# Attention weights turned in front of the last pair's values and copied behind its first four products

## The chip, the cores and the metric

The kernel runs on one core of a Trainium2 chip. Its engines work side by side, each through its own queue in order: TensorE (PE in the rows; PEld are its weight loads), VectorE (DVE), ScalarE (ACT), GpSimd (POOL) and SyncE (SP), which here only issues DMAs. TensorE writes to PSUM; VectorE and ScalarE read PSUM and write SBUF. The metric is the device time of one execution in microseconds, median of several runs.

## What is computed

Three stages on fp32 data: attention that is causal by blocks of 64, for 4 x 8 heads of 576 positions with 64 features; a two-layer network with a leaky ReLU; and a mixture of eight experts whose gate is normalised eight times by rows and columns. The change touches the attention alone:

```python
batch, n_heads, seq, head_dim = (4, 8, 576, 64)

def _attn_ref(q, k, v):
    B, H, S, D = q.shape
    block = 64
    scale = 1.0 / np.sqrt(D)
    scores = scale * np.matmul(q, k.transpose(0, 1, 3, 2))
    pos = np.arange(S)
    mask = pos[:, None] // block >= pos[None, :] // block
    scores = np.where(mask, scores, -1000000000.0)
    scores = scores - np.max(scores, axis=-1, keepdims=True)
    attn = np.exp(scores)
    attn = attn / (np.sum(attn, axis=-1, keepdims=True) + 1e-09)
    return np.matmul(attn, v).astype(np.float32)
```

## The kernel before

The attention works on pairs of heads: 16 pairs, 128 partitions each (two heads of 64). `attention` runs a loop over pairs p from -1 to 16, and in it over the nine query blocks i in the order 8, 7, 0, 6, 1, 5, 2, 4, 3 (`turn_order`). In turn p it works for several pairs at once: the scores of pair p+1, the turning of the weights of pair p, the values of pair p-1, and the loading and turning of q and k for the pairs behind.

- **Score i** (`score`, L323 to L332): one matmul `sc` of 64(i+1) keys (two halves of 288 for score 8), its row maximum on VectorE (`nmax`), and its exponential on ScalarE (`ex`) with the row sum, which is read out by a second short instruction. The PSUM pool of the scores has three buffers. There are ten score matmuls in a turn, so each takes the buffer of the one three before it, once that one's exponential is through.
- **Turning the weights** (`turn_attn`, L358 to L372): the 25 blocks of 128 keys by 128 (two heads of 64 queries) of `ex` are transposed in seven groups, 0 to 6, of four blocks (one in group 6), into a PSUM tile `tr`, and each group is copied into the SBUF tile `at`. Groups 0, 3 and 5 are copied by ScalarE, groups 1, 2, 4 and 6 by VectorE (for pair 15: 0, 2, 4, 6 by ScalarE). Turned q (`qm`), k (`km`) and their tails (`qk_tail`) use the same three PSUM buffers as `tr`. There is one `at` for all pairs.
- **Values** (`weigh`, L385 and L388): twelve products of v with `at`, two heads side by side, into `av`. The first four (all with key chunk 0) read the blocks of groups 0 and 1 and the first of group 2; the other eight read groups 2 to 6.
- **split_x** (L396 to L406): VectorE multiplies `av` by the reciprocal row sums into `xs`; ScalarE casts `xs` to `xh` (two casts for the four pairs whose rows lie in two tiles), and GpSimd takes the rest into `xl`.

The copy of group 0 of pair p overwrites what the first products of pair p-1 have read, so it comes behind them. In the table `beside`, which says what else is written down beside each score, the values, `split_x` and `turn_attn` of group 0 stand beside score 7, groups 1 and 2 beside scores 0 and 6, group 3 beside score 2, group 4 beside 4, and groups 5 and 6 beside 3.

TensorE executes in the order in which the code is written down. On the other engines the scheduler of the framework sets the order from the same code. In the first 15 turns five steps each of preparing the first layer's weights (`bits_steps`, L154 to L202) are mixed in, on VectorE, ScalarE and GpSimd. Everything behind the attention (matmuls at L499, L519, L775, L829) is untouched.

Of the kernel before, what the change touches and what calls it, by code (L numbers as in the profile page):

```python
# [8 lines left out]
F32 = mybir.dt.float32  # L9
# [6 lines left out]
P = 128  # L16
BLK = 64
# [19 lines left out]
def block_attention_mlp_moe(  # L37
# [177 lines left out]
    def attention(att, ps_sc, ps_tr, ps_av):  # L215
        qraw = att.tile([P, NFULL, P], F32, name="qraw")
        kraw = att.tile([P, NFULL, P], F32, name="kraw")
# [16 lines left out]
        order = [(i, c) for c in range(NKC) for i in range(2 * c, NQ)]  # L234
# [115 lines left out]
        def spread_totals(p):  # L350
            with ExitStack() as queued:
                queued.enter_context(tc.issue_after(getattr(fetched[0], "ins", fetched[0])))
                for h in range(2):
                    nc.sync.dma_start(
                        out=by_feature[p % 2][h * D:(h + 1) * D, :], in_=rows[p][h:h + 1, :].to_broadcast([D, S])
                    )

        def turn_attn(p, g):  # L358
            todo = order[4 * g:4 * g + 4]
            n = len(todo)  # L360
            tr = ps_tr.tile([P, 4, 2, BLK], F32, name="tr", tag="tr")
            for s, (i, c) in enumerate(todo):
                nc.tensor.transpose(  # L363
                    tr[:, s].rearrange("p h q -> p (h q)"),
                    ex[p % 2][:, off[i] + c * P:off[i] + (c + 1) * P],
                    ident,
                )
            dst = at[:, 4 * g:4 * g + n]
            if g in ((0, 3, 5) if p + 1 < NP else (0, 2, 4, 6)):
                nc.scalar.copy(out=dst, in_=tr[:, 0:n])  # L370
            else:
                nc.vector.tensor_copy(out=dst, in_=tr[:, 0:n])  # L372
# [20 lines left out]
        def split_x(p):  # L393
# [16 lines left out]


        tails_far = [("far", load_tail, qraw, q), ("far", load_tail, kraw, k)]
        values = [("prv", weigh, 0, h, part) for part in range(2) for h in range(2)]
        values += [("prv", weigh, c, h, 1) for c in range(1, NKC) for h in range(2)]
        beside = {
            8: [("fol", turn_q), ("far", load_rows, qraw, q)],
            7: [("fol", turn_k), ("far", load_rows, kraw, k), *values, ("prv", split_x), ("cur", turn_attn, 0)],
            0: [("cur", turn_attn, 1)],
            6: [("cur", turn_attn, 2), ("nxt", load_v)],
            1: [],  # L420
            5: [("fol", turn_tail), *tails_far],
            2: [("cur", turn_attn, 3)],
            4: [("cur", turn_attn, 4), ("cur", spread_totals)],
            3: [("cur", turn_attn, 5), ("cur", turn_attn, 6)],
        }
        turn_order = [8, 7, 0, 6, 1, 5, 2, 4, 3]

# [95 lines left out]
    with (  # L523
        tc.tile_pool(name="att", bufs=1) as att,
        tc.tile_pool(name="ps_sc", bufs=3, space=bass.MemoryType.PSUM) as ps_sc,
        tc.tile_pool(name="ps_tr", bufs=3, space=bass.MemoryType.PSUM) as ps_tr,
        tc.tile_pool(name="ps_av", bufs=1, space=bass.MemoryType.PSUM) as ps_av,
    ):
        with tc.manual_schedule(engines={mybir.EngineType.PE}):
            attention(att, ps_sc, ps_tr, ps_av)  # L530
# [345 lines left out]
    for m, (r, b, f, first, last) in enumerate(todo):  # L876
# [11 lines left out]
        if r + 1 == len(runs):  # L888
            k = f - first
# [66 lines left out]
    order = [*range(TC // 2, TC), *range(TC // 2)]  # L956
    turned = False
    for n in range(0, NGR, 2):
        p, e, i = groups[n]
# [74 lines left out]
```

## Time and profile before

| | us |
|---|---|
| median of 3 runs | 2105.89 (2105.85 to 2106.43) |
| the profiled execution | 2106.03 |
| its span | 2104.2 |
| TensorE busy in the span | 2095.8 |
| VectorE busy | 1428.0 |
| ScalarE busy | 898.3 |
| start of the values of pair 0 / of pair 15 | 28.18 / 201.72 |

The attention stage ends at 204.57, where the first matmul of L499 starts. A busy TensorE is not a TensorE at its peak: the ends of its matmuls are modelled, and a matmul that follows another overlaps it. So its rows are best read from start to start: what passes between two starts more than the work needs is waiting. The rows of PEld name what a weight load waited for.

### The profile page before, as it was taken

What the parts mean: (1) busy time and instruction counts of PE and PEld (TensorE: products, weight loads), DVE (VectorE), ACT (ScalarE), POOL (GpSimd) and SP (SyncE); (2) the same over time, 40 slices, a digit from 0 to 9 for tenths busy, and PEclk for the clock granted to TensorE, in tenths of its full rate; (3) what the DMA queues carried; (4) which work ended last, traced back from release to release, by engine and by line L of the source; (5) the groups of instructions that cost most, each with busy time, mean ns of one, the idle gap of its engine ahead of it and who ended that gap; (6) DMA issues with size and microseconds to landing.
All of it is one profiled execution on the core that took longest, in us unless ns stands there. A gap on an engine that the chain in (4) does not pass through costs nothing.

```text
span 2104.2 us, 28785 instructions
## 1 busy us (share of the span) xinstructions
PE 2095.8 (100%) x10776; PEld 1846.2 (88%) x10776; DVE 1428.0 (68%) x2321; ACT 898.3 (43%) x1859; POOL 478.3 (23%) x526
## 2 busy tenths in 40 slices
PE   9999999999999999999999999999999999999999
PEld 6666898988899899899899889989989988998998
DVE  7786656565468766766777676676678667667665
ACT  7776332222344443443453444344345344434432
POOL 2222212131003212221222221222122122122210
PEclk9999999999999999999999999999999999999999
DMA  5542111010022212212212221221222222122120
GB/s 139 131 121 75 41 40 51 31 56 25 1 61 81 72 49 81 81 41 80 81 60 91 81 71 51 81 81 41 80 81 82 69 80 72 50 81 81 41 81 30
DMA packets 153533, 142.99 MB, mean 68 GB/s; under 512 B 65073, under 2 KB 122417, under 8 KB 153393
## 3 DMA queue, kind: packets, MB, share of 16 engines
q1 hardware_dynamic: 152192, 140.86, 22.5%
q8 instruction: 84, 1.38, 0.3%
q14 instruction: 57, 0.46, 0.1%
q10 hardware_dynamic: 1200, 0.30, 0.1%
HBM read 136.33 MB, written 4.79 MB: 67 GB/s over the span
## 4 chain that ended last, share of the span: by engine, by line
PE 97%; DVE 1%; DMA 0%; ACT 0%; issue 0%; SPq 0%; DVEq 0%; ACTq 0%
PE o L829 37%; PE h_ps L775 33%; PE h_ps L499 9%; PE o L519 9%; PE sc L323 3%; PE av L388 2%; PE tr L363 1%; DVE xs L396 1%; DVE nmax L324 0%; ACT ex L332 0%; DMA qraw<-in_q_dram 0%; DVE at L372 0%; PE qm L297 0%; PE km L303 0%; PE l_ps L633 0%; PE av L385 0%
## 5 line engine op out<-in xcount | busy, mean ns | idle before, releaser
L829 PE MATMUL o<-w2h,xhlate 128*128 128x512 f32 x1152 | 402.6, 390 | 0.0
L829 PE MATMUL o<-w2h,xllate 128*128 128x512 f32 x1152 | 401.6, 389 | 0.0
L783 ACT COPY s<-h_ps 128x384 f32<-128x384 f32 x288 | 138.0, 480 | 555.1 <-PE h_ps L775 555.0
L792 DVE TENSOR_TENSOR c<-h_ps,s 128x384 f32<-128x384 f32 x288 | 155.8, 554 | 313.1 <-PE h_ps L775 303.2
L716 POOL TENSOR_TENSOR wa<-wraw 128x256 f32<-128x256 f32 x96 | 88.0, 917 | 1170.6 <-DVE w1l L734 1144.3
L775 PE MATMUL h_ps<-xhS,w1h 128*128 128x384 f32 x768 | 257.1, 335 | 0.0
L775 PE MATMUL h_ps<-xlS,w1h 128*128 128x384 f32 x768 | 256.5, 334 | 0.0
L775 PE MATMUL h_ps<-xhS,w1l 128*128 128x384 f32 x768 | 256.5, 334 | 0.0
L829 PEld LDWEIGHTS o<-w2h,xllate 128*128 128x128 f32 x1152 | 216.2, 188 | 45.5
L829 PEld LDWEIGHTS o<-w2h,xhlate 128*128 128x128 f32 x1152 | 216.2, 188 | 43.4
L829 PE MATMUL o<-w2l,xhlate 128*128 128x512 f32 x576 | 224.7, 390 | 0.0
L829 PE MATMUL o<-w2l,xllate 128*128 128x512 f32 x576 | 224.4, 390 | 0.0
L842 DVE SCALAR_TENSOR_TENSOR xa<-o,pr,xa 128x512 f32<-128x512 f32 x264 | 189.2, 741 | 50.1 <-PE o L829 50.1
L775 PE MATMUL h_ps<-xhA,w1l 128*128 128x384 f32 x576 | 193.0, 335 | 0.0
L775 PE MATMUL h_ps<-xhA,w1h 128*128 128x384 f32 x576 | 193.0, 335 | 0.0
L775 PE MATMUL h_ps<-xlA,w1h 128*128 128x384 f32 x576 | 192.7, 335 | 0.0
L734 DVE TENSOR_TENSOR w1l<-wraw,w1h 128x512 fp32r<-128x512 f32 x192 | 172.6, 936 | 1.5 <-ACT w1h L733 1.5
L734 DVE TENSOR_TENSOR w1l<-wa,w1h 128x512 fp32r<-128x512 f32 x192 | 160.4, 838 | 0.2 <-ACT w1h L733 0.2
L798 ACT ACTIVATE xllate<-c 128x384 fp32r<-128x384 f32 x144 | 75.7, 526 | 184.1 <-DVE c L792 184.1
L775 PEld LDWEIGHTS h_ps<-xhS,w1h 128*128 128x128 f32 x768 | 144.2, 188 | 0.1
L775 PEld LDWEIGHTS h_ps<-xlS,w1h 128*128 128x128 f32 x768 | 144.2, 188 | 0.0
L775 PEld LDWEIGHTS h_ps<-xhS,w1l 128*128 128x128 f32 x768 | 144.1, 188 | 0.0
(155 smaller groups left out, 3995.6 us busy)
## 6 DMA issues: line engine op xcount, KB each, us to landing
wraw<-in_moe_w_dram SPq DMA_DIRECT2D x192, 512.0 KB, 4.3
wraw<-in_moe_w_in_dram SPq DMA_DIRECT2D x16, 512.0 KB, 3.7
wraw<-in_moe_w_out_dram SPq DMA_DIRECT2D x16, 512.0 KB, 3.6
by_feature<-row SPq DMA_DIRECT2D x32, 144.0 KB, 3.2
out_dram<-xa SPq DMA_DIRECT2D x18, 256.0 KB, 2.0
qraw<-in_q_dram SPq DMA_DIRECT2D x32, 128.0 KB, 2.8
vraw<-in_v_dram SPq DMA_DIRECT2D x32, 128.0 KB, 2.5
kraw<-in_k_dram SPq DMA_DIRECT2D x30, 128.0 KB, 3.2
```

The costliest lines, as they stand in the source:

```text
L323: nc.tensor.matmul(sc, qbd[p % 2][:, i, :], kT[p % 2][:, lo:hi], start=True, stop=True)
L388: nc.tensor.matmul(av[p][r, 512 + P * max(c - 1, 0):512 + S - P], lhsT, a[:, q0:, :], start=c == 0, stop=c == NKC - 1,)
L499: nc.tensor.matmul(ps[:, 0:n], w[:, c, cols], x, start=c == 0 and s == 0, stop=c == KC - 1 and s == 2,)
L519: nc.tensor.matmul(ps[:, 0:n], w[:, cut], h[:, 0:n], start=start and m == 0, stop=stop and m == 2)
L716: nc.gpsimd.tensor_tensor(out=one[:, 0], in0=a21, in1=a22, op=ALU.add)
L734: nc.vector.tensor_tensor(out=lo, in0=x, in1=f32(hi), op=ALU.subtract)
L775: mm = nc.tensor.matmul(ps, w[:, c], x[:, c], start=first and c == 0 and s == 0, stop=c == 1 and s == 2, skip_group_check=True,)
L783: nc.scalar.copy(out=t, in_=bank[n, name][:, 0:HT])
L792: nc.vector.tensor_tensor(out=c, in0=x, in1=part[n, add], op=ALU.add)
L798: nc.scalar.activation(out=hi, in_=x, func=AF.Relu),
L829: mm = nc.tensor.matmul(o, h, w, start=m == 0, stop=m == 11)
L842: nc.vector.scalar_tensor_tensor(out=a, in0=o, scalar=pr[:, tt, e:e + 1], in1=a, op0=ALU.mult, op1=ALU.add)
```

## The change

`turn_attn` is cut in two: `turn_attn` only transposes a group, and the new `keep_attn` copies it into `at`. Groups 0 and 1 are transposed in front of the values of the pair before, and their copies are written down behind the first four products of these values, in front of the other eight. The groups behind them stand one place later: group 2 beside score 6, 3 beside 5, 4 beside 2, 5 beside 4, 6 beside 3. The engines that copy are the same, and no instruction is added or taken away.

```diff
+        turned_ps = {}
+
         def turn_attn(p, g):
             todo = order[4 * g:4 * g + 4]
             n = len(todo)
-            tr = ps_tr.tile([P, 4, 2, BLK], F32, name="tr", tag="tr")
+            tr = turned_ps[p, g] = ps_tr.tile([P, 4, 2, BLK], F32, name="tr", tag="tr")
             for s, (i, c) in enumerate(todo):
...
+
+        def keep_attn(p, g):
+            n = len(order[4 * g:4 * g + 4])
+            tr = turned_ps.pop((p, g))
             dst = at[:, 4 * g:4 * g + n]
...
+        def turns(*gs):
+            return [("cur", f, g) for g in gs for f in (turn_attn, keep_attn)]
+
         values = [("prv", weigh, 0, h, part) for part in range(2) for h in range(2)]
+        values += [("cur", keep_attn, g) for g in range(2)]
         values += [("prv", weigh, c, h, 1) for c in range(1, NKC) for h in range(2)]
...
-            7: [("fol", turn_k), ("far", load_rows, kraw, k), *values, ("prv", split_x), ("cur", turn_attn, 0)],
-            0: [("cur", turn_attn, 1)],
...
+            7: [("fol", turn_k), ("far", load_rows, kraw, k), ("cur", turn_attn, 0), ("cur", turn_attn, 1),
+                *values, ("prv", split_x)],
+            0: [],
...
```

On TensorE, from the turned k of one pair to score 6 behind the values, the order before is this (a number behind an x counts equal rows in a row; four transpositions are a group, a score of 64(i+1) columns is score i):

```order
L303 MATMUL km<-ident,kraw 128x128 x4
L385 MATMUL av<-at,vraw_107 64x128 x2
L388 MATMUL av<-at,vraw_107 64x448 x4
L388 MATMUL av<-at,vraw_107 64x320 x2
L388 MATMUL av<-at,vraw_107 64x192 x2
L388 MATMUL av<-at,vraw_107 64x64 x2
L363 MATMUL tr<-ident,ex_112 128x128 x4
L323 MATMUL sc<-kT_111,qbd_109 128x64
L363 MATMUL tr<-ident,ex_112 128x128 x4
L323 MATMUL sc<-kT_111,qbd_109 128x448
L363 MATMUL tr<-ident,ex_112 128x128 x4
```

And now:

```order
L303 MATMUL km<-ident,kraw 128x128 x4
L365 MATMUL tr<-ident,ex_112 128x128 x8
L391 MATMUL av<-at,vraw_107 64x128 x2
L394 MATMUL av<-at,vraw_107 64x448 x4
L394 MATMUL av<-at,vraw_107 64x320 x2
L394 MATMUL av<-at,vraw_107 64x192 x2
L394 MATMUL av<-at,vraw_107 64x64 x2
L323 MATMUL sc<-kT_111,qbd_109 128x64
L323 MATMUL sc<-kT_111,qbd_109 128x448
L365 MATMUL tr<-ident,ex_112 128x128 x4
L323 MATMUL sc<-kT_111,qbd_109 128x128
```

Eight transpositions, groups 0 and 1, have moved from behind the values to in front of them; the two scores that were between the groups follow the values directly.

On TensorE behind that, from score 1 to score 8 of the next pair, before:

```order
L323 MATMUL sc<-kT_111,qbd_109 128x128
L323 MATMUL sc<-kT_111,qbd_109 128x384
L308 MATMUL qk_tail<-ident,tails 128x128
L323 MATMUL sc<-kT_111,qbd_109 128x192
L363 MATMUL tr<-ident,ex_112 128x128 x4
L323 MATMUL sc<-kT_111,qbd_109 128x320
L363 MATMUL tr<-ident,ex_112 128x128 x4
L323 MATMUL sc<-kT_111,qbd_109 128x256
L363 MATMUL tr<-ident,ex_112 128x128 x5
L323 MATMUL sc<-kT_110,qbd_108 128x288 x2
```

And now:

```order
L323 MATMUL sc<-kT_111,qbd_109 128x128
L323 MATMUL sc<-kT_111,qbd_109 128x384
L308 MATMUL qk_tail<-ident,tails 128x128
L365 MATMUL tr<-ident,ex_112 128x128 x4
L323 MATMUL sc<-kT_111,qbd_109 128x192
L365 MATMUL tr<-ident,ex_112 128x128 x4
L323 MATMUL sc<-kT_111,qbd_109 128x320
L365 MATMUL tr<-ident,ex_112 128x128 x4
L323 MATMUL sc<-kT_111,qbd_109 128x256
L365 MATMUL tr<-ident,ex_112 128x128
L323 MATMUL sc<-kT_110,qbd_108 128x288 x2
```

Group 3 has moved in front of score 2, group 4 in front of score 4 and group 5 in front of score 3; group 6 alone stands last.

On ScalarE, from the copy of group 0 to the exponential of score 3, before (an exponential of 64(i+1) columns is that of score i):

```order
L370 COPY at<-tr 128x512
L405 CAST xhfirst<-xs 128x576
L332 ACTIVATE ex_112,ssum_116<-sc,nmax_114 128x64
L332 ACTIVATE ex_112,ssum_116<-sc,nmax_114 128x448
L289 ACTIVATE qbd_109<-qk_tail 64x64 x2
L332 ACTIVATE ex_112,ssum_116<-sc,nmax_114 128x128
L332 ACTIVATE ex_112,ssum_116<-sc,nmax_114 128x384
L332 ACTIVATE ex_112,ssum_116<-sc,nmax_114 128x192
L370 COPY at<-tr 128x512
L332 ACTIVATE ex_112,ssum_116<-sc,nmax_114 128x320
L370 COPY at<-tr 128x512
L332 ACTIVATE ex_112,ssum_116<-sc,nmax_114 128x256
```

And now:

```order
L376 COPY at<-tr 128x512
L411 CAST xhfirst<-xs 128x576
L332 ACTIVATE ex_112,ssum_116<-sc,nmax_114 128x64
L332 ACTIVATE ex_112,ssum_116<-sc,nmax_114 128x448
L332 ACTIVATE ex_112,ssum_116<-sc,nmax_114 128x128
L289 ACTIVATE qbd_109<-qk_tail 64x64 x2
L376 COPY at<-tr 128x512
L332 ACTIVATE ex_112,ssum_116<-sc,nmax_114 128x384
L332 ACTIVATE ex_112,ssum_116<-sc,nmax_114 128x192
L376 COPY at<-tr 128x512
L332 ACTIVATE ex_112,ssum_116<-sc,nmax_114 128x320
L332 ACTIVATE ex_112,ssum_116<-sc,nmax_114 128x256
```

The copy of group 3 has moved in front of the exponentials of scores 5 and 2, and the copy of group 5 in front of that of score 4; the cast of xs still stands in front of the exponential of score 0. On VectorE the copy of group 1 has moved from behind `xs` and the maximum of score 0 to in front of `xs`.

## Rows read from the trace of the kernel before

**Rows 1.** Stretches of 20 us: length, busy us (pieces) of PE, PEld, DVE, ACT, POOL, clock, DMA.

```profile
0.00:20.00 20.00, 16.76 (x83) 11.85 (x84) 12.06 (x37) 12.00 (x36) 6.21 (x25) 1.00 0.73 178
...
280.00:300.00 20.00, 20.00 (x117) 19.86 (x116) 11.30 (x18) 6.42 (x13) 5.19 (x4) 1.00 0.17 53
```

**Rows 2.** Chain of waits, one interval: start us, length us, what.

```profile
105.53 0.60 DVE at L372
...
106.78 0.73 ACT ex L332 x2
```

**Rows 3.** Timeline, TensorE, one interval: start, busy us, what [idle before, releaser].

```profile
100.68 0.60 PE L303 MATMUL km<-ident,kraw 128*128 128x128 f32 x4
...
101.21 0.44 PE L385 MATMUL av<-at,vraw 128*64 128x128 f32 x4
...
104.06 0.66 PE L363 MATMUL tr<-ident,ex 128*128 128x128 f32 x4
...
104.55 0.33 PE L323 MATMUL sc<-kT,qbd 128*128 128x64 f32 x2
...
104.72 0.61 PE L363 MATMUL tr<-ident,ex 128*128 128x128 f32 x4
...
105.17 0.92 PE L323 MATMUL sc<-kT,qbd 128*128 128x448 f32 x2
...
106.36 1.03 PE L323 MATMUL sc<-kT,qbd 128*128 128x128 f32 x4
...
107.23 0.27 PE L308 MATMUL qk_tail<-ident,tails 128*128 128x128 f32 x1
...
107.56 0.30 PEld L323 LDWEIGHTS sc<-kT,qbd 128*128 128x128 f32 x2 [0.51 <-ACT ex L332]
...
107.99 0.60 PE L363 MATMUL tr<-ident,ex 128*128 128x128 f32 x4
...
108.52 0.30 PEld L323 LDWEIGHTS sc<-kT,qbd 128*128 128x128 f32 x2 [0.17 <-ACT ex L332]
...
110.03 0.71 PE L363 MATMUL tr<-ident,ex 128*128 128x128 f32 x5
...
110.58 1.14 PE L323 MATMUL sc<-kT,qbd 128*128 128x288 f32 x4
...
111.55 0.60 PE L297 MATMUL qm<-ident,qraw 128*128 128x128 f32 x4
...
112.85 0.60 PE L303 MATMUL km<-ident,kraw 128*128 128x128 f32 x4
```

**Rows 4.** Timeline, VectorE and ScalarE, the same interval.

```profile
104.20 1.19 DVE L396 TENSOR_TENSOR xs<-av,by_feature 128x576 f32<-128x576 f32 x1 [1.34 <-PE av L388]
...
105.43 0.67 ACT L405 CAST xhfirst<-xs 128x576 fp32r<-128x576 f32 x1
...
106.22 0.19 ACT L332 ACTIVATION_READ_ACCUMULATOR ex<-sc,nmax 128x1 f32 x1
...
109.89 0.53 ACT L332 ACTIVATE ex<-sc,nmax 128x320 f32<-128x320 f32 x1
...
110.31 0.19 ACT L332 ACTIVATION_READ_ACCUMULATOR ex<-sc,nmax 128x1 f32 x1
...
110.72 0.58 ACT L370 COPY at<-tr 128x512 f32<-128x512 f32 x1 [0.22 <-PE tr L363]
...
111.20 0.48 ACT L332 ACTIVATE ex<-sc,nmax 128x256 f32<-128x256 f32 x1
...
112.19 1.19 ACT L289 ACTIVATE qbd<-qm 64x512 f32<-64x512 f32 x2 [0.41 <-PE qm L297]
```

**Rows 5.** Timeline of an interval whose cast of xs is in two parts.

```profile
142.92 0.19 ACT L332 ACTIVATION_READ_ACCUMULATOR ex<-sc,nmax 128x1 f32 x1
...
142.96 1.12 PE L323 MATMUL sc<-kT,qbd 128*128 128x128 f32 x4
```

**Rows 6.** Timeline, the last transpositions of the stage.

```profile
198.37 3.42 PE L363 MATMUL tr<-ident,ex 128*128 128x128 f32 x25
```

More of the change, by code (lines that the diff above doesn't have):

```diff
@@ L416, in attention @@
             8: [("fol", turn_q), ("far", load_rows, qraw, q)],
-            7: [("fol", turn_k), ("far", load_rows, kraw, k), *values, ("prv", split_x), ("cur", turn_attn, 0)],
-            0: [("cur", turn_attn, 1)],
-            6: [("cur", turn_attn, 2), ("nxt", load_v)],
+            7: [("fol", turn_k), ("far", load_rows, kraw, k), ("cur", turn_attn, 0), ("cur", turn_attn, 1),
+                *values, ("prv", split_x)],
+            0: [],
+            6: [*turns(2), ("nxt", load_v)],
             1: [],
[L421 to L424, printed above, removed]
+            5: [("fol", turn_tail), *tails_far, *turns(3)],
+            2: [*turns(4)],
+            4: [*turns(5), ("cur", spread_totals)],
+            3: [*turns(6)],
         }
```

## The prediction

> **What bounds the kernel now.** I read the stretches of 20 us first. Behind the attention stage (the first 204 us, where the change lies) TensorE is busy for 20.00 of 20 us [rows 1], and the chain that ended last is TensorE's own there; nothing has room to swallow or give back time, so what the stage gains or loses reaches the end one to one. In the attention stage the same pattern comes once per pair. I count it from the start of one turning of k (km, 100.68) to the next (112.85): 12.17 us [rows 3]. Behind a pair's values the chain of waits leaves TensorE: it goes over xs, a copy of weights, a maximum and an exponential and comes back at a score; two of its pieces stand in [rows 2].
>
> The timeline of TensorE in that interval shows where it stands still. Between starts, five transpositions take 0.55 (110.03 to 110.58), so a group of four 0.44, and scores 1 and 5 together 0.87 for 512 columns, so 0.21 for score 1 and 0.64 for score 5. What a score takes goes by its columns. The tail transposition alone should take 0.11, but 0.33 pass until score 2 begins, and its weight load names the exponential as what it waited for; score 2 itself takes 0.43 where 192 columns are worth 0.32. The same again at score 4: 0.53 instead of 0.43 in front of it [rows 3]. Score 2 and score 4 need the buffer of the score three before them (three PSUM buffers), so scores 6 and 1, and their exponentials are late because the maximum of score 6 stands on VectorE behind xs and the copy of group 1 [rows 2]. These waits are what the change can win.
>
> **What the change moves on TensorE.** It turns groups 0 and 1 in front of the twelve products of values instead of behind them, and interleaves the later groups one place later. No matmul is added or taken away, so the work of TensorE stays. Groups 0 and 1 are ready there: their input was finished in the interval before, and the buffer of group 1 is free when the spread of q ends, at 112.19 + 1.19, which is 0.53 after km [rows 3, 4]; group 1 would come 0.86 after km. No cost.
>
> **What the copies win.** The copies of groups 0 and 1 need the first four products only, about the first 0.96 of the 2.85 us that the values take (1,152 of 3,200 columns, two halves of the array at a time). VectorE idles 1.34 us in front of xs [rows 4], so the copy of group 1 (0.60 in the chain, [rows 2]) fits there, and the maximum of score 6 no longer stands behind it. With that, the waits of scores 2 and 4 go: 0.22 + 0.11 in front of and in score 2, 0.10 + 0.11 for score 4, 0.06 at group 0, and 0.06 in small gaps: **0.66 us per interval** to be won.
>
> **First new wait: score 5.** Score 5 takes the buffer of score 0. That is free when score 0's exponential has ended, which on ScalarE stands behind the cast of xs, which waits for xs, which waits for the last product of the values. In the trace this runs: xs begins with the end of the values at 104.20, the cast at 105.43, and the accumulator of score 0's exponential is read out at 106.22 + 0.19 = 106.41; a waiting TensorE goes on 0.06 later, as at score 2 (106.78 + 0.73 = 107.51, started 107.56). So from TensorE's first start behind the values (104.06) to the earliest start of score 5 there are 2.41 us [rows 2 to 4]. Today TensorE has 2.51 of work there (group 0, score 0, group 1, score 6, group 2, score 1: 106.36 + 0.21 - 104.06), 0.10 more than needed. The change takes both groups out of this stretch. What is left is score 0 with 0.17 (104.55 to 104.72), score 6 and group 2 with 1.19 (105.17 to 106.36) and score 1 with 0.21, together 1.57. The chain is untouched, since the order on ScalarE still has the cast of xs in front of the exponential of score 0, and on VectorE xs in front of its maximum. Wait: 2.41 - 1.57 = **0.84**, and behind a wait the weight load is not covered, **0.11** as in score 2. That the buffer really binds is seen in the four intervals where the cast is split in two: there the accumulator ends at 142.92 + 0.19 = 143.11, and scores 1 and 5, which began at 142.96, last 1.12 instead of 1.03 [rows 3, 5]: with score 5 ready at 142.96 + 0.21 and released at 143.17 there is no cover left, and the first hundredths over it are already felt.
>
> **Second new wait: second half of score 8.** It takes the buffer of score 4. On ScalarE the exponential of score 4 now stands behind the copy of group 5, where it stood in front of it. Group 5 is turned behind score 4: from its start on TensorE to its copy on ScalarE pass 0.69 (110.03 to 110.72), the next instruction begins 0.48 later (111.20), the exponential of score 4 with its accumulator takes 0.61 (109.89 to 110.31 + 0.19) and the release 0.06: 1.84 us [rows 3, 4]. TensorE has by then group 5, score 3, group 6 and the first half of score 8: 0.43 + 0.43 + 0.11 + 0.48 = 1.45. Wait **0.39**, weight load **0.11**. The exponential of score 5 moves behind the copy of group 3 in the same way. Score 3 needs it. From the start of score 5: 0.86 to group 3, 0.69 to its copy, 0.48 to the exponential, at most the 0.73 of score 6's until that is out, 0.06: 2.82. TensorE's way to score 3 is 0.75 + 0.11 + 0.43 + 0.32 + 0.44 + 0.53 + 0.43 = 3.01. No wait, 0.19 to spare.
>
> **The interval:** + 0.95 + 0.50 - 0.66 = **+0.79 us**, 12.96 instead of 12.17. There are 13 such intervals (pairs 1 to 13): 10.3 us. The first interval has no values and no xs, but the second wait; bounds are none and one whole 0.79, I take 0.3. Pair 14 has the first wait and loses its own waits at scores 2 and 4 (0.95 - 0.55): +0.4. At the end, pair 15's group 0 now stands straight behind pair 14's last groups, and its fourth transposition needs the exponential of score 3, last on ScalarE: 0.69 + 0.48 + 0.52 + 0.57 + 0.06 = 2.32 after group 5's start, where TensorE is there after 1.29: wait 1.03, load 0.11. Groups 0 and 1 (0.86) come out of the 3.42 us of transpositions between the last two runs of values [rows 6]; the 17 that stay there need 1.9, and an estimate with the copy of group 3 behind xs is 2.3: 1.14 + 0.86 - 1.1 = +0.9. Sum: 10.3 + 0.3 + 0.4 + 0.9 = **11.9 us**. The profiled execution took 2106.03 (span 2104.2 and 1.83 around it), 0.14 over the median; the end of the stage shifts, the rest does not, so 2105.89 + 11.9 = **2117.8 us**.
>
> The queue of SP changes by a line: the row of totals goes out ahead of the second load of q. Both have most of an interval until they are needed, so nothing. The last step of w preparation on VectorE in front of xs has 1.34 us of idle time to share with the copy, also nothing; without that cover the copy would cost 0.60 per interval on top, which I keep for the upper end.
>
> [...] In the rows the weight load of score 2 starts with the release and its products last 0.43 instead of 0.32 [rows 3]. [...] The row is of the very kind of instruction, a score that waits for its buffer, so I keep 0.11.
>
> **Rivals.** *Only the first wait is there:* score 8 isn't held, because ScalarE reaches the copy of group 5 without delay. Then an interval costs 0.29, 3.8 in all, and with the opening and the end near nothing 2109.7. Against it: the copy can't start before group 5 is turned, and that alone makes the 1.84. *Only the second:* an interval gains 0.16, about 2104.5; for that the chain of 2.41 would have to shrink by 0.84. *Faster:* the copies leave the tail of the values, the waits of scores 2 and 4 go, and nothing takes their place, because score 0's buffer comes free in time. That is 0.6 per interval, 14 times 8.4 us: 2097.5. It decides at score 5: xs, cast and exponential would have to be through 1.57 us after the values, and they take 2.41; only an exponential of score 0 ahead of the cast on ScalarE and a maximum ahead of xs on VectorE would do it, and neither is in the order. *Longer waits:* the copy of group 1 delays xs, or the first interval and the end cost double: 0.3 more per interval, about 2122. [...]
>
> **How the numbers follow.** Both waits: 0.75, 2117.8, its own range 2115 to 2121. Only the first: 0.08. Only the second: 0.05. Faster: 0.06. Longer: 0.05. Clock: 0.01. The range 2110 to 2122 takes in the first with both ends of the weight load, half of "longer" and the upper part of "only the first". A measurement of this kernel tells 0.2%, 4.2 us, from no change. Slower by more than that: 0.75 + 0.05 + 0.01 and half of "only the first", 0.85. Within: the other half and "only the second", 0.09. Faster: 0.06.
>
> **What would show it.** In the profile after, the interval from km to km should be near 12.96. The weight load of score 5 should wait for the exponential and start some 6.65 after km; the second half of score 8 should wait for the exponential of score 4, about 1.84 after group 5 starts; scores 2 and 4 should follow their predecessors without a wait. On VectorE the copy of group 1 should lie in front of xs and end before it. If score 5 starts 5.8 after km, the first step is wrong, and the kernel is not slower by this; if the second half of score 8 starts 0.48 behind the first, the second is.

## The result and the profile after

| | us |
|---|---|
| median after | 2118.03 (2117.47 to 2118.53, 6 runs) |
| median before, same chip | 2106.24 (2105.85 to 2107.98, 6 runs) |
| ratio, 95% interval | 1.0055 (1.0042 to 1.0068) |
| span of the profiled execution | 2116.0 (before 2104.2) |
| values of pair 0 to the end of the attention | from km at 27.54 to 216.34 (before 27.65 to 204.57) |

The change makes the kernel slower by 11.8 us. The page has TensorE ahead as before, with 97% of the chain that ended last, and its clock shows no dip.

```profile
PE 2097.5 (99%) x10776; PEld 1847.4 (87%) x10776; DVE 1431.2 (68%) x2321; ACT 895.1 (42%) x1859; POOL 478.2 (23%) x526
...
PEclk9999999999999999999999999999999999999999
...
PE 97%; ACT 1%; DMA 1%; DVE 1%; issue 0%; POOL 0%; ACTq 0%; SPq 0%; DVEq 0%
```

TensorE's timeline in the interval that answers to [rows 3] (start, busy us, what, idle time and releaser). From km to km it is now 12.99 us (105.74 to 118.73), where it was 12.17:

```profile
105.74 0.60 PE L303 MATMUL km<-ident,kraw 128*128 128x128 f32 x4
106.18 1.04 PE L365 MATMUL tr<-ident,ex 128*128 128x128 f32 x8
107.14 0.44 PE L391 MATMUL av<-at,vraw 128*64 128x128 f32 x4
...
110.00 1.24 PE L323 MATMUL sc<-kT,qbd 128*128 128x64 f32 x4
111.07 0.60 PE L365 MATMUL tr<-ident,ex 128*128 128x128 f32 x4
111.51 0.39 PE L323 MATMUL sc<-kT,qbd 128*128 128x128 f32 x2
...
112.39 0.30 PEld L323 LDWEIGHTS sc<-kT,qbd 128*128 128x128 f32 x2 [0.69 <-ACT ex L332]
...
113.14 0.27 PE L308 MATMUL qk_tail<-ident,tails 128*128 128x128 f32 x1
113.25 0.60 PE L365 MATMUL tr<-ident,ex 128*128 128x128 f32 x4
113.69 0.49 PE L323 MATMUL sc<-kT,qbd 128*128 128x192 f32 x2
...
115.00 0.60 PE L365 MATMUL tr<-ident,ex 128*128 128x128 f32 x4
...
115.97 0.65 PE L323 MATMUL sc<-kT,qbd 128*128 128x288 f32 x2
...
116.84 0.30 PEld L323 LDWEIGHTS sc<-kT,qbd 128*128 128x128 f32 x2 [0.68 <-ACT ex L332]
...
117.44 0.60 PE L297 MATMUL qm<-ident,qraw 128*128 128x128 f32 x4
...
118.73 0.27 PE L303 MATMUL km<-ident,kraw 128*128 128x128 f32 x1
```

Score 1 begins at 111.51 and is worth 0.21, so score 5 could begin at 111.72; its weights are loaded at 112.39, when an exponential lets it go: a wait of 0.67. The second half of score 8 could begin 0.48 behind the first, at 116.45; it begins at 116.84: 0.39. Both then pay an uncovered weight load: score 5 lasts 0.75 to the tail instead of 0.64, and the second half of score 8 0.60 to qm instead of 0.48. From the tail to group 3 pass 0.11 and from there to score 2 0.44, so the waits of scores 2 and 4 are gone.

VectorE and ScalarE in the same interval, answering to [rows 4]:

```profile
108.38 0.69 DVE L378 COPY at<-tr 128x512 f32<-128x512 f32 x1 [0.45 <-PE av L394]
...
110.14 1.19 DVE L402 TENSOR_TENSOR xs<-av,by_feature 128x576 f32<-128x576 f32 x1 [1.06 <-DMA kraw<-in_k_dram]
...
111.36 0.67 ACT L411 CAST xhfirst<-xs 128x576 fp32r<-128x576 f32 x1 [2.34 <-DVE xs L402]
111.94 0.31 ACT L332 ACTIVATE ex<-sc,nmax 128x64 f32<-128x64 f32 x1
112.15 0.19 ACT L332 ACTIVATION_READ_ACCUMULATOR ex<-sc,nmax 128x1 f32 x1
...
115.69 0.59 ACT L376 COPY at<-tr 128x512 f32<-128x512 f32 x1 [0.18 <-PE tr L365]
116.17 0.53 ACT L332 ACTIVATE ex<-sc,nmax 128x320 f32<-128x320 f32 x1
116.59 0.20 ACT L332 ACTIVATION_READ_ACCUMULATOR ex<-sc,nmax 128x1 f32 x1
```

The copy of group 1 lies between the first four products and xs, as the change means it to. Score 5 starts 0.05 behind 112.15 + 0.19, the end of the accumulator read-out of score 0's exponential, which stands behind xs and the cast. The second half of score 8 starts 0.05 behind 116.59 + 0.20, 1.84 behind the start of group 5 (115.00). In the list of waits between 28 and 187 us this is one line (us in total, times, longest), which was 9.4, 27, 0.6 before:

```profile
PEld sc L323 <- ACT ex L332: 17.0, 24, 1.0
```

### The profile page after: what moved, and what is told of

Read it like the earlier page. It is cut to its first block, busy times and chain, and to the rows that moved or that the text cites. A ratio compares the mean times of both kernels' runs of the same rounds, so it can differ in the third digit from the quotient of the medians.

```text
span 2116.0 us, 28793 instructions
## 1 busy us (share of the span) xinstructions
PE 2097.5 (99%) x10776; PEld 1847.4 (87%) x10776; DVE 1431.2 (68%) x2321; ACT 895.1 (42%) x1859; POOL 478.2 (23%) x526
## 4 chain that ended last, share of the span: by engine, by line
PE 97%; ACT 1%; DMA 1%; DVE 1%; issue 0%; POOL 0%; ACTq 0%; SPq 0%; DVEq 0%
PE o L840 37%; PE h_ps L786 33%; PE h_ps L510 9%; PE o L530 9%; PE sc L323 3%; PE av L394 2%; PE tr L365 2%; DMA vraw<-in_v_dram 1%; ACT ex L332 1%; ACT at L376 0%; DVE xs L402 0%; PE qm L297 0%; PE av L391 0%; PE km L303 0%; PE l_ps L644 0%; DMA qraw<-in_q_dram 0%
```

## The experiments

Ratios are to the kernel before on the same chip, with 95% intervals. An interval is again km to km, in the plain pairs (one cast of xs); the kernel before has 12.17, the changed one 13.00.

**1. The two halves of the change, each alone.** The first run turns groups 0 and 1 in front and leaves the later groups where they were; the second leaves groups 0 and 1 behind the values and moves the later groups only.

Against the changed kernel, the first:

```diff
-            5: [("fol", turn_tail), *tails_far, *turns(3)],
-            2: [*turns(4)],
-            4: [*turns(5), ("cur", spread_totals)],
-            3: [*turns(6)],
+            5: [("fol", turn_tail), *tails_far ],
+            2: [*turns(3)],
+            4: [*turns(4), ("cur", spread_totals)],
+            3: [*turns(5, 6)],
```

The second:

```diff
-        values += [("cur", keep_attn, g) for g in range(2)]
...
-            7: [("fol", turn_k), ("far", load_rows, kraw, k), ("cur", turn_attn, 0), ("cur", turn_attn, 1),
-                *values, ("prv", split_x)],
-            0: [],
+            7: [("fol", turn_k), ("far", load_rows, kraw, k), *values, ("prv", split_x), *turns(0)],
+            0: [*turns(1)],
```

> One half of the change: groups 0 and 1 are turned in front of the values and copied behind the first four products, groups 3 to 6 stay where the kernel before has them, so that ScalarE has the exponential of score 4 in front of the copy of group 5 again. Theory (two waits for score buffers, 0.94 us at score 5 and 0.51 at the second half of score 8 in each of 13 intervals): the second wait goes, the first stays; an interval of 12.49 us, total about 2111 us. Rival A (the copies beside the values slow the products): nothing comes back, 2118. Rival B (the first wait alone makes the loss, the second is absorbed): 2118.

> The other half of the change alone: groups 0 and 1 stay behind the values, groups 3 to 6 stand one place later, in front of scores 2, 4 and 3. Theory: no wait at score 5 (its cover is back), the wait of 0.51 at the second half of score 8 is there, and the waits of 0.54 at scores 2 and 4 of the kernel before go, since a group stands in front of each; an interval of about 12.13 us, total 2105 to 2107 us. Rival A (copies beside the values): 2106, without any wait at score 8. Rival B (the first wait alone): below 2100, since the second wait would cost nothing.

Measured: front only 2111.52 us, 1.0026 (1.0015 to 1.0036), 12.49 per interval; shift only 2105.89, 1.0000 (0.9990 to 1.0009), 12.22. In the first, score 5 alone waits long; in the second, the second half of score 8 does (1.39 from score 8 to qm, where 0.97 is its work). Either new wait thus belongs to its half of the change. The halves do not add up to the whole (5.5 and 0 against 11.8), because the old waits can be won only once. By difference the whole wins 0.61 of them per interval (0.94 + 0.50 of new waits, 0.83 longer), the first half about as much (0.91 of new wait, 0.32 longer), the second 0.37 (0.42 of new wait, 0.05 longer); experiment 3 shows why not more. The products of the values take 2.86 in the changed kernel (107.14 to 110.00) and 2.85 before (101.21 to 104.06), so the copies beside them do not slow them.

**2. The second wait.** The changed kernel with the copies of groups 4 and 5 swapped between the engines:

```diff
-            if g in ((0, 3, 5) if p + 1 < NP else (0, 2, 4, 6)):
+            if g in ((0, 3, 4) if p + 1 < NP else (0, 2, 4, 6)):
```

> The changed kernel with the copies of groups 4 and 5 exchanged between the engines: ScalarE copies group 4, VectorE group 5. The exponential of score 4 then no longer stands behind the copy of group 5. Theory: the second half of score 8 does not wait, 0.51 less per interval, 12.49 us, total about 2111 us; score 5 waits as before. Rival A and rival B: 2118.

Measured: 2114.96 us, 1.0044 (1.0027 to 1.0061), 12.70 per interval. Of 0.50 only 0.30 came back. ScalarE's copy of group 4 and exponential of score 4, and the weight load of the second half of score 8, in an interval of that kernel:

```profile
113.89 0.59 ACT L376 COPY at<-tr 128x512 f32<-128x512 f32 x1
114.35 0.56 ACT L332 ACTIVATE ex<-sc,nmax 128x320 f32<-128x320 f32 x1
114.77 0.23 ACT L332 ACTIVATION_READ_ACCUMULATOR ex<-sc,nmax 128x1 f32 x1
...
115.05 0.30 PEld L323 LDWEIGHTS sc<-kT,qbd 128*128 128x128 f32 x2 [0.38 <-ACT ex L332]
```

No idle time stands in front of the copy or of the exponential: the copy of group 4 costs the exponential of score 4 its time in ScalarE's queue, where that of group 5 had cost it a wait for TensorE. The next run has both copies on VectorE:

```diff
-            if g in ((0, 3, 5) if p + 1 < NP else (0, 2, 4, 6)):
+            if g in ((0, 3) if p + 1 < NP else (0, 2, 4, 6)):
```

> The changed kernel with the copies of groups 4 and 5 both on VectorE. When only 4 and 5 were swapped, 0.30 of the 0.50 of the second wait came back, and ScalarE ran without a pause up to the exponential of score 4. If ScalarE's queue (the copy of 0.5 in front of that exponential) is what kept the other 0.20, it goes now: no wait at the second half of score 8, 12.50 per interval, 13 x 0.50 = 6.5 off, about 2111.5. The rival: VectorE, which then copies five groups of seven, holds the maximum of score 4 behind the copies; then 12.70 or more per interval, 2115 or above.

Measured: 2112.74 us, 1.0031 (1.0019 to 1.0043), 12.59 per interval. 0.41 of 0.50 came back; the remaining 0.09 is the same load, released too late to be covered: its exponential now idles 0.27 for its maximum, which stands behind the copy of group 4 on VectorE and starts 0.81 behind score 4, where with that copy on ScalarE it was 0.74. ScalarE's queue was the cause, and VectorE is the next in line by a little. As a control the same copy was moved in the kernel before:

> A control: the kernel before with the copies of groups 5 (and 4, which is there already) on VectorE. If the copies off ScalarE help only where the second half of score 8 waits for the exponential of score 4, there is nothing to win here: 12.17 per interval, within 0.1, 2105 to 2107. If ScalarE's load as such holds the attention stage, it wins here as well: 12.0 or below, 2103 or less.

Measured: 2105.71 us, 0.9999 (0.9990 to 1.0008), 12.17. A lighter ScalarE is worth nothing where no score waits behind the copy.

**3. The first wait.** In the changed kernel xs is queued behind the maximum of score 3, and its cast behind the exponential of score 3:

```diff
+        def split_late(p):
+            with ExitStack() as queued:
+                if p + 2 < NP:
+                    for x in (latest[0], heads[1]):
+                        queued.enter_context(tc.issue_after(getattr(x, "ins", x)))
+                split_x(p)
...
-                *values, ("prv", split_x)],
+                *values],
...
-            3: [*turns(6)],
+            3: [("prv", split_late), *turns(6)],
```

(`latest[0]` is the last maximum, `heads[1]` the last exponential.)

> The changed kernel with xs queued on VectorE behind the maximum of score 3 and its cast on ScalarE behind the exponential of score 3 (issue order alone). The exponential of score 0 then no longer stands behind them. Theory: score 5 does not wait, 0.94 less per interval, about 12.06 us, the wait at the second half of score 8 stays; total about 2105 us. Rival A (copies beside the values): 2118. A third reading, that the maxima behind xs are late anyway, would leave a wait at score 2 in its place: above 2110.

Measured: 2108.81 us, 1.0013 (1.0004 to 1.0023), 12.31 per interval. Score 5 no longer waits; score 8 still does, until 1.85 behind group 5. Rows of one interval:

```profile
106.67 0.53 PEld L324 LDWEIGHTS sc<-kT,qbd 128*128 128x128 f32 x4
...
108.69 0.19 ACT L333 ACTIVATION_READ_ACCUMULATOR ex<-sc,nmax 128x1 f32 x1
...
108.94 0.30 PEld L324 LDWEIGHTS sc<-kT,qbd 128*128 128x128 f32 x2
108.96 0.79 PE L324 MATMUL sc<-kT,qbd 128*128 128x320 f32 x2
...
111.43 0.30 PEld L324 LDWEIGHTS sc<-kT,qbd 128*128 128x128 f32 x2 [0.60 <-ACT ex L333]
```

The four loads from 106.67 are scores 1 and 5, without a pause between them. So the first wait hangs on xs and the cast. Of 0.94 expected, 0.69 came back: 0.16 of the rest still passes from score 0 to group 2 (1.08 where the pieces are worth 0.92). Most of the other 0.09 comes from scores 4 and 3: the load of score 4 starts 0.06 behind the accumulator read-out of score 1 (108.69 + 0.19), almost too late to be covered, and score 4 lasts 0.62 (108.96 to 109.58) and score 3 0.51, 0.07 more each than in the changed kernel, while the wait of score 8 gets 0.08 shorter. No idle time of TensorE shows this. The shift-only kernel has the same (0.63 and 0.51), so score 4's load is no better covered there than before (0.64).

**4. Both waits out, and no gain.** Three runs that were to take the old and the new waits away together. The first is the front-only kernel with xs late, the second the kernel before with xs late:

```diff
-            3: [*turns(5, 6)],
+            3: [("prv", split_late), *turns(5, 6)],
...
-            3: [("cur", turn_attn, 5), ("cur", turn_attn, 6)],
+            3: [("prv", split_late), ("cur", turn_attn, 5), ("cur", turn_attn, 6)],
```

The third is the first with group 2 between scores 0 and 6:

```diff
-            0: [],
-            6: [*turns(2), ("nxt", load_v)],
+            0: [*turns(2)],
+            6: [("nxt", load_v)],
```

> Groups 0 and 1 in front of the values, groups 3 to 6 at their old places, and xs queued behind the maximum of score 3 with its cast behind the exponential of score 3. My theory, that the first new wait (score 5 for score 0's buffer behind xs and the cast) and the second one (second half of score 8) are the whole loss: neither has its cause here, and the waits of scores 2 and 4 are gone as well. The front-only kernel had 12.49 per interval, and xs behind score 3 took 0.69 back in the changed kernel: 12.49 - 0.69 = 11.80 per interval, and with pair 14 about 2111.5 - 14 x 0.69 = 2101.9, clearly faster than the kernel before. A rival: the cast, now between the exponentials of score 3 and of the next score 8, holds the exponentials of the next pair back, and a new wait comes at score 7 or behind it; then the interval stays at 12.2 or above, 2106 or more.

> The kernel before, with nothing turned in front; xs alone is queued behind the maximum of score 3 and its cast behind the exponential of score 3. If the waits of scores 2 and 4 come from xs in front of the maximum of score 6, as I read it, they go without the change: 12.17 - 0.60 = 11.57 per interval, and 14 x 0.60 = 8.4 off: 2097.7; then the change's turning in front was not needed for its gain. The rival: the copy of group 1, which still stands in front of the maximum of score 6, makes those waits by itself; then about half stays, 11.85 per interval, 2101.7.

> As the run with groups 0 and 1 in front and xs behind score 3, but group 2 turned between score 0 and score 6 and not behind score 6. In the changed kernel 1.08 passed from score 0 to group 2, where score 0 and score 6 are worth 0.92; I put the 0.16 to score 6's weight load, which the short score 0 (64 columns) does not cover. If so, group 2 behind score 0 and score 6 behind a full transposition take the 0.16 out: 0.16 less per interval than in that run, 11.64 if that is 11.80, and some 2.1 us less. If the 0.16 belongs to score 0 itself (its own short length), it stays, and both runs have the same interval.

Measured, in this order: 2109.75 us, 1.0020 (1.0011 to 1.0030), 12.38 per interval; 2106.72, 1.0003 (0.9994 to 1.0012), 12.17; 2113.21, 1.0034 (1.0021 to 1.0047), 12.57. All three missed, and the misses overturn a reading of mine. These are rows of TensorE, VectorE and ScalarE of the second, the kernel before with xs late:

```profile
104.99 0.92 PE L324 MATMUL sc<-kT,qbd 128*128 128x448 f32 x2
...
105.94 0.62 DVE L325 TENSOR_REDUCE nmax<-sc 128x1 f32<-128x448 f32 x1
...
106.60 0.64 ACT L333 ACTIVATE ex<-sc,nmax 128x448 f32<-128x448 f32 x1 [1.08 <-DVE nmax L325]
...
107.38 0.30 PEld L324 LDWEIGHTS sc<-kT,qbd 128*128 128x128 f32 x2 [0.51 <-ACT ex L333]
...
110.56 1.18 DVE L397 TENSOR_TENSOR xs<-av,by_feature 128x576 f32<-128x576 f32 x1
```

xs has gone to 110.56, and yet score 2 waits as long as before. The maximum of score 6 begins 0.95 behind score 6's start, as in the kernel before, where score 6 starts at 105.17 [rows 3]:

```profile
105.92 0.60 PE L363 MATMUL tr<-ident,ex 128*128 128x128 f32 x4
...
106.12 0.62 DVE L324 TENSOR_REDUCE nmax<-sc 128x1 f32<-128x448 f32 x1
```

The copy of group 1 still stands in front of the maximum in the second run. In the first, neither xs nor that copy does:

```profile
107.03 0.60 PE L366 MATMUL tr<-ident,ex 128*128 128x128 f32 x4
...
107.23 0.62 DVE L325 TENSOR_REDUCE nmax<-sc 128x1 f32<-128x448 f32 x1 [0.58 <-PE sc L324]
...
108.66 0.30 PEld L324 LDWEIGHTS sc<-kT,qbd 128*128 128x128 f32 x2 [0.51 <-ACT ex L333]
```

VectorE idles 0.58 for score 6, and its maximum begins 0.20 behind the start of group 2, the next work of TensorE, just as it did before; score 2's load idles for the same 0.51. So nothing in front of this maximum delays it.

In the second run it is 2.39 from the start of score 6 to score 2 (104.99 to 107.38), and in [rows 3] it is the same 2.39 (105.17 to 107.56). That is score 6's own way through maximum, exponential and accumulator, and TensorE has only group 2, scores 1 and 5 and the tail in between. The third run shows it by taking group 2 out of that way, 0.44 of work:

```profile
107.81 1.79 PE L324 MATMUL sc<-kT,qbd 128*128 128x448 f32 x6
109.44 0.27 PE L308 MATMUL qk_tail<-ident,tails 128*128 128x128 f32 x1
110.20 0.59 PE L324 MATMUL sc<-kT,qbd 128*128 128x192 f32 x2 [0.49 <-ACT ex L333]
```

From score 6 to score 2 again 2.39 (107.81 to 110.20), and from the tail to score 2 now 0.76 instead of 0.33: 0.43 more. So the waits of scores 2 and 4 go when TensorE is kept longer in between, not when xs or a copy leaves VectorE. In the shift-only kernel it is group 3, now in front of score 2, that does it; in the front-only one it is the wait of score 5, and the changed kernel has both. The first of the three lost its wait at score 5 and got these two back for it.

The third run also answers for the 0.16: from score 0 to the tail it has 2.34 (107.10 to 109.44), the first 2.38 (105.95 to 108.33). Only 0.04 went. Score 0 alone still takes 0.27 to group 2, where in [rows 3] it takes 0.17 behind group 0. The 0.16 is thus mostly score 0's start straight behind the values, and not the weight load of score 6.

**5. A version that beats both.** If the shift alone takes the old waits away, and its one new wait hangs on ScalarE's copies, the shift without the turning in front and with both copies on VectorE should win (the second diff of experiment 1 and the second of experiment 2):

> Groups 0 and 1 stay behind the values, the later groups stand one place later, and the copies of groups 4 and 5 go to VectorE (only 0 and 3 stay on ScalarE). My theory now: the waits of scores 2 and 4 go by the place of group 3 alone (it puts 0.44 of work between score 6 and score 2), and what that shift costs is only the wait of the second half of score 8. The shift alone had 12.22 per interval, of which 0.42 is that wait (1.39 from score 8 to qm instead of 0.97), and in the changed kernel the copies off ScalarE took 0.42 back: 12.22 - 0.42 = 11.80, 13 intervals 5.5 us, 2105.9 - 5.5 = 2100.4, faster than before by some 0.26%. The rival: VectorE, which has xs in front of the maxima here as before, gets so late with the two further copies that the exponentials of scores 5 and 4 come no earlier; then 12.2 or above, 2105 to 2107.

Measured: 2100.50 us, 0.9974 (0.9964 to 0.9984), 11.81 per interval (86.14 to 97.95). The list of waits of that kernel, between 28 and 187 us, has one wait of a score left for an exponential (the list shows idle time only: scores 4 and 3 last 0.63 and 0.50 here, as in experiment 3), and the end of the attention comes at 198.99:

```profile
PEld sc L323 <- ACT ex L332: 0.6, 1, 0.6
...
198.99 0.50 PE L508 MATMUL h_ps<-xhfirst,w1h 128*128 128x512 f32 x1
```

The changed kernel itself with both of its waits treated (the diff of experiment 3 and the second of experiment 2):

> The changed kernel with both new waits treated: xs behind the maximum of score 3, its cast behind the exponential of score 3, and the copies of groups 4 and 5 on VectorE. If the two waits are independent of each other, the gains add: xs late alone came to 12.31, copies off ScalarE alone took 0.42: 12.31 - 0.42 = 11.89 per interval, 2108.8 - 5.5 = 2103.3, a little faster than before. If TensorE only runs into the next wait, xs and its cast hold score 8 or the q of the next pair: then 12.1 or above, 2106 or more.

Measured: 2109.62 us, 1.0018 (1.0009 to 1.0027), mostly 12.38 per interval. The wait of score 8 is gone, but group 1, in front of the values, now waits. TensorE and ScalarE there:

```profile
101.85 0.60 PE L366 MATMUL tr<-ident,ex 128*128 128x128 f32 x4
102.71 0.66 PE L366 MATMUL tr<-ident,ex 128*128 128x128 f32 x4 [0.26 <-ACT qbd L289]
...
100.89 0.67 ACT L412 CAST xhfirst<-xs 128x576 fp32r<-128x576 f32 x1 [0.54 <-DVE xs L403]
101.47 1.19 ACT L289 ACTIVATE qbd<-qm 64x512 f32<-64x512 f32 x2
```

Group 1 needs the buffer of qm, which the spread of q frees at 101.47 + 1.19 = 102.66, and the late cast stands in front of that spread. From group 0 to group 1 pass 0.86 instead of 0.44: 0.42, just what the copies had won. The rival that TensorE only runs into the next wait was right.

## Why the prediction was right, and where it was not

**The time.** 2117.8 was forecast for the likeliest case and 2118.03 measured. Per interval 12.96 was forecast and 13.00 came (13.08 in the four with two casts; one interval, 66.49 to 79.76, took 13.27).

**First new wait: right in place, time and cause.** Score 5's load starts 6.65 behind km (105.74 to 112.39), as forecast, released by the exponential of score 0. The wait is 0.67 and not 0.84, because TensorE comes to it 0.16 later than the sum had it; 0.67 + 0.16 + 0.11 is 0.94 against 0.95. The queueing of xs behind score 3 takes it away (experiment 3).

**Second new wait: right in all its terms.** 1.84 from group 5 to the second half of score 8 was forecast and is measured, 0.39 of wait and 0.11 of load likewise. Experiment 2 adds why a swap of the copies does not undo all of it.

**The uncovered load** of 0.11 behind a wait stands in both new waits in the rows of after (0.75 for 0.64, 0.60 for 0.48). There the load of the score begins with the release: 112.39 for score 5, which starts at 112.39, and 116.84 for the second half of score 8, which starts at 116.85. Score 1, which does not wait, starts at 111.51, 0.11 behind its load (111.40). Of the "both ends of the weight load" in the forecast, the end with no load to pay behind a wait for a buffer is shown by no run.

**What the change wins: the size was about right, the step that names its cause was wrong.** The prediction's bounds say the exponentials of scores 6 and 1 are late because the maximum of score 6 stands behind xs and the copy of group 1, and the part on the copies lets the waits of scores 2 and 4 go because the copies leave. Experiment 4 shows that nothing stood in front of that maximum that mattered: with xs and the copy gone it begins no earlier behind score 6. The chain of waits in the kernel before goes through the copy of group 1, which ends at 106.13 (105.53 + 0.60), when the maximum begins; but score 6 itself ends at 106.09 by its row (105.17 + 0.92), so the two came within hundredths of each other, and taking the copy away frees nothing. What was won, 0.61 by difference where 0.66 was forecast, came from group 3 in front of score 2, or from the wait of score 5 in front of both. The sum came out since it goes by the time that TensorE stood still, whatever ended it, and that the same edit moved group 3 as well was luck for this step. As a guide to a better kernel the step misled: the first two runs of experiment 4, built on it, missed by 8 and 9 us.

**"No cost" of the turning in front** held for its own place (km to values 1.40 with both groups; 0.53 before, and 0.94 for the groups behind the values). It left out 0.16 at scores 0 and 6, which the wait of score 5 swallows; without that wait it is a cost. The front-only kernel with xs late, which has the old waits too, takes 12.38 against 12.17: 0.16 of this is at scores 0 and 6, and the rest is group 1, held behind the late cast (km to values 1.52). In the changed kernel group 1's buffer was in time as forecast; experiment 5 shows how little room there is.

**Opening and end.** The first km with values comes 0.11 earlier (27.65 to 27.54): the interval in front of it is 0.28 longer, but the turning of q in front of that starts 0.40 earlier (16.48 to 16.08), with its loads. The forecast of 0.3 was a guess between two bounds and came out by luck: score 5 waits in this interval too (0.41 idle in front of 21.26), which the forecast had left out, as there is no xs. The twelve intervals to 184.05 are 10.11 longer (156.51 against 146.40; 9.5 forecast). From there to the end of the stage 1.77 more passes (32.29 against 30.52; 0.79 + 0.4 + 0.9 = 2.1 forecast): 0.36 instead of 0.79 in the last interval of the 13 (184.05 to 196.61, before 174.05 to 186.25), and 1.41 behind it, 1.3 forecast. No q is turned at the end of that interval, and score 7's load idles 0.57 there in the kernel before, 0.16 now: the new wait of score 8 partly stands in for an old one. Together 11.77, and the span is 11.8 longer. The last transposition of pair 15's group 0 waits for the exponential of score 3 and starts 2.31 behind group 5 (205.32), 2.32 forecast:

```profile
207.63 0.77 PE L365 MATMUL tr<-ident,ex 128*128 128x128 f32 x5 [0.84 <-ACT ex L332]
208.32 0.44 PE L391 MATMUL av<-at,vraw 128*64 128x128 f32 x4
...
211.17 2.39 PE L365 MATMUL tr<-ident,ex 128*128 128x128 f32 x17
213.49 0.44 PE L391 MATMUL av<-at,vraw 128*64 128x128 f32 x4
```

The 17 transpositions that stay between the last two runs of values take 2.32 to the next values, 2.3 forecast.

**Rivals.** "Only the first" and "only the second" were built as kernels (experiment 1): 2111.5 and 2105.9, not 2109.7 and 2104.5; in the changed kernel both waits are there. "Faster" needed score 0's buffer 1.57 behind the values, and it came at 2.39 (110.00 to 112.39). The clock stayed at 1.00 in every stretch of 20 us of the first 300 after. A lower clock, with 0.01 in the forecast, was the author's estimate, and no run shows one: the mean granted clock of every execution was 0.999 or 1.000.

**Open.** The interval of 13.27: the copy of group 5 begins 0.97 behind group 5 (75.74 to 76.71) instead of 0.69, and the shift-only kernel has the same 0.97 in the same pair (72.44 to 73.41, interval 12.51). That it comes at the same pair in two kernels speaks against chance; what holds the copy there no row shows.

## What to carry to other kernels

A matmul that reuses a PSUM buffer has a whole way to wait for, here 2.39 us for a score of 448 columns in three kernels: the earlier matmul's columns, its maximum, its exponential, its accumulator. What counts is how much work TensorE has between the two, so a move of work out of such a stretch is priced as lost cover there, and a move into it as a gain, before anything else. When the releaser of a wait is known, ask of each step of its way whether it idled for something that can be moved; if the step began as soon as its input was out, taking its neighbours in the queue away wins nothing, even where the chain of waits runs through them. And with several waits in a ring of three buffers, one that is removed lets the next come up: price the next before counting the gain.

## What the runs showed of the hardware

A score that waited for its buffer did not load its weights ahead: the load started 0.05 to 0.06 behind the end of the accumulator read-out, in every such wait above. Where TensorE stood waiting, some 0.11 of the load was seen; where the release came just before its turn, 0.07 to 0.09 (scores 3 and 4 in experiment 3, where no row shows idle time, and score 8 with both copies on VectorE). A score 0 straight behind the values took 0.27 to the next start, and 0.17 behind a group of transpositions; why, these runs don't say. Waits of 0.67 and 0.39 in each 13 us left the granted clock at 1.00, with TensorE busy for 18.6 to 19.1 of 20 us between 20 and 200 us, here in one of these stretches:

```profile
60.00:80.00 20.00, 18.63 (x113) 13.02 (x114) 15.58 (x39) 15.06 (x49) 4.72 (x7) 1.00 0.38 89
```

(Columns as in [rows 1].)
